# An mLSTM cell with a multiplicative FFN on one core: transposes of y, k and q moved from TensorE to VectorE

## Chip, cores, metric

One core of a Trainium2 chip. The metric is device time of one execution in microseconds (us), lower is better.

## The reference

```python
# mLSTM cell: batch 4, heads 8, 768 tokens, head dimension 40
for t in range(S):
    m_new = np.maximum(f_gate[:, :, t] + m, i_gate[:, :, t])
    C = f_stab * C + i_stab * (v_t outer k_t)        # state per batch and head
    n = f_stab * n + i_stab * k_t
    y[:, :, t] = sigmoid(o_gate_t) * (C @ q_t) / max(|n . q_t|, 1)
x = y.transpose(0, 2, 1, 3).reshape(3072, 320)
# multiplicative FFN, weights in float64
out = ((x @ w1) * (x @ w2) @ w3 @ w_out).astype(np.float32)   # (3072, 320)
```
(The stabilised gates are written in words.)

## The kernel before

The sequence is cut into 24 units of 128 rows of one batch. A loop of 30 steps runs the cell of unit s in step s; y of unit n is formed on VectorE right after the cell matmuls of step n+1, and turned (so that features lie on partitions) for the up-projections some steps later. Beside this, the float64 weights are converted by five VectorE passes a piece, two pieces a step; a piece of w3 is then transposed into `w3T`, and TensorE folds w3 and w_out into one matrix, one `wp` block a step in steps 10 to 17. Steps 17 to 26 each have two output blocks `po`.

TensorE does all transposes: `pt` for k and q, `px` for y.

```python
    def turn(n):                                   # k and q of unit n
        for src, dst, name in ((kbuf[n % NB], kT_t, "kT"), (qbuf[n % NBQ], qT_t, "qT")):
            pt = mps([128, NP, P], "pt")
            for p in range(NP):
                transpose(pt[:, p, :], src[:, 2 * p:2 * p + 2, :].rearrange("p a b -> p (a b)"))
            dst[n] = sb.tile([128, NP, P], FP, name=name, tag=name)
            nc.scalar.copy(out=dst[n], in_=pt)
    # ... cut
    def w3_mm(ko):                                 # one block of w3 times w_out
        w3T = w3T_t.pop(ko)
        wp = mps([128, DM], "wp")
        for ki in range(FO):
            mm(wp, w3T[:, ki, :], wo[:, ki, :], start=(ki == 0), stop=(ki == FO - 1))
        nc.scalar.mul(out=w3o[:, ko, :], in_=wp, mul=UP ** -2)
    # ... cut; the loop of steps, shortened:
    for s in range(len(n_up)):
        # loads for s+2 and s+3 on the SP queue
        if s < NU:
            # ...
            if s:
                turn(s)
        while turned < min(s - 2, NU):
            x_trans(turned)                        # px: y of unit s-3
            turned += 1
        fold()                                     # wp
        for _ in range(n_down[s]):
            ffn_out(*downs.pop(0))                 # po
        now = [ups.pop(0) for _ in range(n_up[s])]
        open_ups = [up(*x) for x in now]           # pa, pb
        if len(now) < 2 and turned == s - 2 < NU:
            x_trans(turned)
            turned += 1
        # ...
        quarter_work(s, rest)                      # ab; cell; pw, state, h, y
        # ...
        for _ in range(n_cvt[s] if s < len(n_cvt) else 0):
            convert()                              # five passes, then w3T
            converted += 1
        while todo and fetched < converted + (2 if s < 2 else 3):
            fetch(*todo.pop(0))                    # next raw weights, SP queue
            fetched += 1
```
TensorE's order is pinned to the order in which the program is written. VectorE's order is not, from step 7 on: the build places its instructions by its own estimate of when their inputs are there.

Of the kernel before, what the change touches and what calls it, by code (L numbers as in the profile page):

```python
# [8 lines left out]
FP = mybir.dt.float32  # L9
# [7 lines left out]
def kernel(  # L17
# [26 lines left out]
    nc = tc.nc  # L44
# [44 lines left out]
    def mm(out, lhsT, rhs, start=True, stop=True):  # L89
        in_order(nc.tensor.matmul(out, lhsT=lhsT, rhs=rhs, start=start, stop=stop))  # L90
# [3 lines left out]

    halves = [slice(0, L), slice(L, P)]
    quarters = ((0, 0), (1, 1), (0, 1), (1, 0))


    NB, NBQ = 4, 3
    qbuf = [const.tile([P, H, DP], FP, name=f"qbuf{i}") for i in range(NBQ)]  # L100
    kbuf = [const.tile([P, H, DP], FP, name=f"kbuf{i}") for i in range(NB)]
# [6 lines left out]
    decay = const.tile([P, B * NP, NT], FP, name="decay")  # L108
    U_d = dram.tile([NT, BH, L], FP, name="U_d")

    o_t, u_t = {}, {}

    def rows(src, n):
        c, b = divmod(n, B)
        return src[b, :, c * P:(c + 1) * P, :].rearrange("h p d -> p h d")

    def load(n):
        for dst, src in ((kbuf[n % NB][:, :, 0:D], k), (qbuf[n % NBQ][:, :, 0:D], q), (vbuf[n % NB][:, :, 0:D], v)):
            nc.sync.dma_start(out=dst, in_=rows(src, n))

# [145 lines left out]

    def turn(n):
        for src, dst, name in ((kbuf[n % NB], kT_t, "kT"), (qbuf[n % NBQ], qT_t, "qT")):
            pt = mps([128, NP, P], "pt")
            for p in range(NP):  # L270
# [3 lines that stand above are left out]
# [12 lines left out]
    def quarter_work(s, rest):  # L286
# [11 lines left out]
        if 0 <= n < NU:  # L298
            pw, vt, qT = u_t.pop(n), vbuf[n % NB], qT_t.pop(n)
            before = before_t.pop(n)  # L300
            for hd in range(H):
                for x, r in enumerate(halves):
                    mm(ph[x][:, hd, :], pw[r, hd, :], vt[r, hd, :])
            for p in range(NP):
                for hip, x in quarters:
                    mm(pi[halves[x], hip, p, :], qT[halves[hip], p, halves[x]], before[x][halves[hip], p, :])
        n, first_read = s, None
        if n < NU:
# [11 lines left out]
            for p in range(NP):  # L320
                for hip, x in quarters:
                    mm(ss[halves[x], hip, p, :], kT[halves[hip], p, halves[x]], qT[halves[hip], p, halves[x]])
            pv = pw.rearrange("p (n two) t -> p two n t", two=2)
# [10 lines left out]
        if 0 <= s - 1 < NU:  # L334
            if first_read is None:
                outputs(s - 1, pi, ph)
            else:
                with tc.issue_after(first_read.ins):
                    outputs(s - 1, pi, ph)

    def outputs(n, pi, ph):
# [6 lines left out]
        for x, r in enumerate(halves):  # L348
# [11 lines left out]
        y_t[n] = sb.tile([P, DM + REM], FP, name="y", tag="y")  # L360
        nc.vector.tensor_tensor(out=y_t[n][:, 0:DM].rearrange("p (h d) -> p h d", d=D), in0=h[:, :, 0:D], in1=e,  # L361
                                op=OP.mult)

    def twice(n):
# [15 lines left out]
    RG = GR * BH  # L380
    f_sb, a, F, U, on = (const.tile([RG, TC], FP, name=n) for n in ("f_sb", "a", "F", "U", "on"))
    w, g = f_sb, on
# [32 lines left out]
    for t in state:  # L415
        nc.gpsimd.memset(t[0], 0.0)
    nc.gpsimd.memset(pick, 0.0)

# [97 lines left out]
    def ffn_out(gr, j):  # L516
        po = mps([P, DM], "po")
        for f in range(FO):
            mm(po, ab_t[gr][j // 2][:, f, j % 2 * P:(j % 2 + 1) * P], w3o[:, f, :], start=(f == 0), stop=(f == FO - 1))
        o_sb = ffn.tile([P, DM], FP, name="o_sb", tag="o_sb", bufs=3)  # L520
        nc.scalar.copy(out=o_sb, in_=po)  # L521
        t0 = j * S + gr * P
        nc.sync.dma_start(out=out[t0:t0 + P, :], in_=o_sb)

# [14 lines left out]
    for s in range(len(n_up)):  # L539
# [8 lines left out]
        if s < NU:  # L548
            weighted(s)
            if s >= B:  # L550
                decayed(state[s % B][1], state[s % B][0], s, 0)
            if s:
                turn(s)
        if 0 <= s - 2 < NU:
            twice(s - 2)
        while turned < min(s - 2, NU):
            x_trans(turned)
            turned += 1
# [4 lines left out]
        open_ups = [up(*x) for x in now]  # L563
        if len(now) < 2 and turned == s - 2 < NU:
            x_trans(turned)
            turned += 1

        def rest():
            for x in open_ups:
                up_rest(*x)  # L570

        if s <= NU:
            quarter_work(s, rest)
        else:
            rest()
        if s == 0:
            gate_cols(g, gT, nc.scalar.copy)
            out_gate(0)
            scale_next()
            weights(1)  # L580
# [3 lines left out]
        if B - 1 <= s < NU:  # L584
            if s + 1 < NU:
                weights(s + 1)
            out_gate(s)
        for _ in range(n_cvt[s] if s < len(n_cvt) else 0):
            convert()
            converted += 1  # L590
        while todo and fetched < converted + (2 if s < 2 else 3):
# [35 lines left out]
```

## Time and profile before

| | before |
|---|---|
| time, median of 4 | 495.28 us (494.52 to 497.24) |
| TensorE busy | 462.7 us, 94% |
| VectorE busy | 247.5 us, 50% |
| a step in 12 to 16 | 16.77 us |
| a step in 18 to 23 | 21.08 us |

The prediction shows the lines that carry the bound. Two more are needed later: what the SP queue, which issues all but three of the transfers that the page lists (274 of 277), waits for. The columns are total us, times, longest us.

```profile
SPq L523 <- ACT o_sb L521: 166.7, 24, 30.8
...
SPq L154 <- DVE ma L173: 36.0, 13, 5.1
```
The first is output rows waiting for their copy, the second raw weights waiting for a buffer that a conversion pass must free.

### The profile page before, as it was taken

The numbers are of one execution on the slowest core, as the hardware profiler recorded it, in microseconds if no ns is written. First come the engines' busy times: TensorE is split into PE (matmuls) and PEld (weight loads), VectorE is DVE, ScalarE is ACT, GpSimd is POOL, SyncE is SP. The second block draws the span as 40 slices with busy tenths as digits, with TensorE's granted clock in tenths as the row PEclk, the third lists the DMA queues.
The fourth block names the chain that finished last, engine by engine and source line by source line (L and its number), as shares of the span: only waits on it lengthen the run. The fifth ranks groups of instructions, "written<-read, shape, count | busy, mean of one in ns | idle before, by whom it ended". The sixth has DMA issues, their size and how long they took to land.

```text
span 494.0 us, 13423 instructions
## 1 busy us (share of the span) xinstructions
PE 462.7 (94%) x5714; PEld 380.6 (77%) x5714; DVE 247.5 (50%) x512; ACT 153.5 (31%) x413; POOL 88.6 (18%) x163
## 2 busy tenths in 40 slices
PE   3869797899899999999999999999999998999997
PEld 2759796898677888788878787777878777777864
DVE  7787688999877978977431331403214042111110
ACT  3743454533431543354331322412112011011011
POOL 5431223621311322212410211201000000000000
PEclk9989998989999999999999999999999999999999
DMA  9999936799877737543340422311000000000001
GB/s 186 169 196 197 155 91 130 124 184 180 156 147 136 156 113 152 103 74 56 53 88 15 102 50 56 65 40 41 15 28 1 27 16 15 27 15 13 1 15 40
DMA packets 115404, 42.33 MB, mean 86 GB/s; under 512 B 103120, under 2 KB 106384, under 8 KB 115344
## 3 DMA queue, kind: packets, MB, share of 16 engines
q1 hardware_dynamic: 115200, 41.37, 41.9%
q8 instruction: 45, 0.74, 0.7%
q14 instruction: 15, 0.12, 0.1%
q10 hardware_dynamic: 144, 0.10, 0.1%
HBM read 37.42 MB, written 4.03 MB: 84 GB/s over the span
## 4 chain that ended last, share of the span: by engine, by line
PE 75%; DVE 9%; issue 7%; DMA 3%; SPq 2%; POOL 2%; ACT 1%; DVEq 0%; POOLq 0%; ACTq 0%
PE po L90 21%; PE pa L90 20%; PE pb L90 14%; PE cell L90 7%; PE wp L90 7%; PE pt L93 3%; SPq L154 2%; DVE h L349 1%; DMA raw<-in_moe_w_dram 1%; DMA pw<-U_d 1%; PE px L93 1%; DMA kbuf<-in_k_dram 1%; PE ub L90 1%; DVE h L345 1%; DVE ma L173 1%
## 5 line engine op out<-in xcount | busy, mean ns | idle before, releaser
L514 DVE TENSOR_TENSOR ab<-pb,a_sb 128x512 f32<-128x512 f32 x48 | 33.0, 690 | 182.0 <-ACT a_sb L513 181.9
L90 PE MATMUL po<-w3o,ab 128*128 128x320 f32 x384 | 105.4, 433 | 1.3 <-DVE h L349 1.3
L90 PEld LDWEIGHTS po<-w3o,ab 128*128 128x128 f32 x384 | 72.2, 190 | 30.7 <-issue 1.5
L90 PE MATMUL pa<-xT,w 128*128 128x256 f32 (+1 forms) x448 | 93.0, 355 | 0.0
L90 PE MATMUL pb<-xT,w 128*128 128x256 f32 (+1 forms) x448 | 91.9, 351 | 0.4 <-issue 0.4
L90 PEld LDWEIGHTS pa<-xT,w 128*128 128x128 f32 x448 | 77.1, 195 | 10.7 <-ACT a_sb L513 0.8
L90 PEld LDWEIGHTS pb<-xT,w 128*128 128x128 f32 x448 | 76.3, 192 | 9.0 <-issue 0.6
L513 ACT ACTIVATE a_sb<-pa 128x512 f32<-128x512 f32 x48 | 28.6, 596 | 146.6 <-PE pb L90 146.6
L90 PE MATMUL pb<-xT,wr 64*64 64x256 f32 (+1 forms) x448 | 47.4, 351 | 0.0
L90 PE MATMUL pa<-xT,wr 64*64 64x256 f32 (+1 forms) x448 | 47.4, 351 | 0.0
L283 POOL TENSOR_TENSOR state<-state,decay 128x164 f32<-128x164 f32 x40 | 19.6, 493 | 154.2 <-PE cell L90 99.1
L264 POOL TENSOR_SCALAR_AFFINE_SELECT pw<-pw 64x512 f32<-64x512 f32 x48 | 36.9, 769 | 47.1 <-ACT pw L262 44.6
L262 ACT ACTIVATE pw<-pw,aT 128x64 f32<-128x64 f32 x160 | 40.6, 339 | 5.3 <-DMA pw<-U_d 5.3
L90 PEld LDWEIGHTS pa<-xT,wr 64*64 64x64 f32 x448 | 28.5, 133 | 14.9 <-issue 6.6
L90 PE MATMUL wp<-wo,w3T 128*128 128x320 f32 x128 | 35.9, 433 | 2.0 <-DVE w3T L223 2.0
L521 ACT COPY o_sb<-po 128x320 f32<-128x320 f32 x24 | 10.2, 426 | 74.8 <-PE po L90 74.7
L90 PEld LDWEIGHTS wp<-wo,w3T 128*128 128x128 f32 x128 | 23.7, 190 | 11.1 <-issue 2.2
L90 PEld LDWEIGHTS cell<-vbuf,pw 64*64 64x64 f32 x768 | 28.2, 145 | 2.8 <-issue 0.3
L90 PEld LDWEIGHTS pb<-xT,wr 64*64 64x64 f32 x448 | 28.5, 133 | 0.0
L90 PE MATMUL cell<-vbuf,pw 64*64 64x41 f32 x768 | 28.4, 235 | 0.0
L365 POOL COPY y<-y 128x64 f32<-128x64 f32 x24 | 7.3, 306 | 110.0 <-DVE y L361 109.8
L324 DVE TENSOR_TENSOR pw<-cell,pw 128x512 f32<-128x512 f32 x24 | 16.4, 685 | 19.0 <-PE cell L90 15.4
(89 smaller groups left out, 524.4 us busy)
## 6 DMA issues: line engine op xcount, KB each, us to landing
raw<-in_moe_w_dram SPq DMA_DIRECT2D x64, 128.0 KB, 3.5
pw<-U_d SPq DMA_DIRECT2D x40, 128.0 KB, 3.7
kbuf<-in_k_dram SPq DMA_DIRECT2D x24, 160.0 KB, 4.6
qbuf<-in_q_dram SPq DMA_DIRECT2D x24, 160.0 KB, 4.9
vbuf<-in_v_dram SPq DMA_DIRECT2D x24, 160.0 KB, 4.9
o_in<-in_o_gate_dram SPq DMA_DIRECT2D x24, 160.0 KB, 4.1
out_dram<-o_sb SPq DMA_DIRECT2D x24, 160.0 KB, 1.8
raw<-in_moe_w_dram SPq DMA_DIRECT2D x7, 512.0 KB, 5.8
```

The costliest lines, as they stand in the source:

```text
L90: in_order(nc.tensor.matmul(out, lhsT=lhsT, rhs=rhs, start=start, stop=stop))
L93: in_order(nc.tensor.transpose(out, in_, ident[0:n, 0:n]))
L154: nc.sync.dma_start(out=dst, in_=src)
L173: V.scalar_tensor_tensor(out=r.bitcast(FP), in0=lo, scalar=2.0 ** -52, in1=r.bitcast(FP), op0=OP.mult, op1=OP.mult)
L262: nc.scalar.activation(out=pw[:, h, :], in_=src[:, h, :], func=AF.Exp, bias=aT[:, c, b * H + h:b * H + h + 1])
L264: nc.gpsimd.affine_select(out=pw[r], in_=pw[r], compare_op=OP.is_ge, fill=0.0, base=0, pattern=[[0, H], [1, L]], channel_multiplier=-1)
L283: nc.gpsimd.tensor_tensor(out=new, in0=old, op=OP.mult, in1=decay[:, b * NP:(b + 1) * NP, 2 * c + x:2 * c + x + 1] .to_broadcast([P, NP, D1]))
L324: first_read = nc.vector.tensor_tensor(out=pv, in0=ss, in1=pv, op=OP.mult)
L365: nc.gpsimd.tensor_copy(out=y_t[n][:, DM:DM + REM], in_=y_t[n][:, KF * P:DM])
L513: nc.scalar.mul(out=a_sb, in_=pa, mul=UP ** -2)
L514: nc.vector.tensor_tensor(out=ab_t[gr][j][:, fs[0]:fs[-1] + 1, t0:t0 + a_sb.shape[-1]], in0=pb, in1=a_sb, op=OP.mult)
L521: nc.scalar.copy(out=o_sb, in_=po)
```

## The change

The intent is to take transposes off TensorE, which is 94% busy, and put them on VectorE, which is half idle. The program has VectorE turn 32x32 blocks (the `r=32` of its rearrangements) and has the blocks moved by transfers: y of units 8 to 23 goes to DRAM and comes back as 32-row blocks, and k and q of units 17 to 23 are loaded that way. The conversion passes are told to follow the x transpose of their step. Output rows go to ScalarE's DMA queue. The diff, cut to its core:

```diff
+    N_DVE = 17
+    NY = 8
+    def send(n):                                  # y to DRAM: 4 DMAs on SP
+    def get_back(n):                              # back as 32-row blocks: 4 DMAs on SP
+        back_t[n] = sb.tile([P, 4, KC, 32], FP, name="yb", tag="yb", bufs=1)
+    def x_turn(n):
+        return nc.vector.transpose(out=x_t[gr][...], in_=back_t.pop(n)...)
     def turn(n):
+        if n >= N_DVE:                            # k, q by VectorE
+            nc.vector.transpose(out=dst[n]..., in_=src[...]...)
+            return
-                    mm(pi[...], qT[halves[hip], p, halves[x]], before[x][halves[hip], p, :])
+                    mm(pi[...], qT[heads[hip], p, halves[x]], before[x][heads[hip], p, :])   # 40 rows, not 64
-        nc.sync.dma_start(out=out[t0:t0 + P, :], in_=o_sb)
+        nc.scalar.dma_start(out=out[t0:t0 + P, :], in_=o_sb)
-        if 0 <= s - 2 < NU:
-            twice(s - 2)
+        if NY <= s - 2 < NU:
+            send(s - 2)
+        elif 0 <= s - 2 < NY:
+            twice(s - 2)
+        if N_DVE <= s + 1 < NU:
+            load_turned(s + 1)
+        if NY <= s - 2 < NU:
+            get_back(s - 2)
-        if len(now) < 2 and turned == s - 2 < NU:
+        if len(now) == 1 and turned == s - 2 < NY:
-            quarter_work(s, rest)
+            gated = quarter_work(s, rest)         # returns the instruction y
+        with tc.issue_after(gated.ins) if gated else nullcontext():
+            if NY <= s - 2 < NU:
+                gated = x_turn(s - 2)
+            if N_DVE <= s + 1 < NU:
+                turn(s + 1)
-        for _ in range(n_cvt[s] if s < len(n_cvt) else 0):
-            convert()
+        with tc.issue_after(gated.ins) if gated else nullcontext():
+            for _ in range(n_cvt[s] if s < len(n_cvt) else 0):
+                convert()
```
`issue_after` keeps what stands in it behind the named instruction. `o_sb` goes from 3 to 2 buffers.

More of the change, by code (lines that the diff above doesn't have):

```diff
@@ L1 @@
-from contextlib import ExitStack
+from contextlib import ExitStack, nullcontext
 import concourse.bass as bass
@@ L95 @@
     halves = [slice(0, L), slice(L, P)]
+    heads = [slice(0, D), slice(DP, DP + D)]
     quarters = ((0, 0), (1, 1), (0, 1), (1, 0))
     NB, NBQ = 4, 3
+    N_DVE = 17
     qbuf = [const.tile([P, H, DP], FP, name=f"qbuf{i}") for i in range(NBQ)]
@@ L109 @@
     U_d = dram.tile([NT, BH, L], FP, name="U_d")
+    NY = 8
+    KC = KF + 1
+    y_d = [dram.tile([P, 4, KC, 32], FP, name=f"y_d{n}") if n >= NY else None for n in range(NU)]
     o_t, u_t = {}, {}
@@ L118, in load, with load_turned @@
         for dst, src in ((kbuf[n % NB][:, :, 0:D], k), (qbuf[n % NBQ][:, :, 0:D], q), (vbuf[n % NB][:, :, 0:D], v)):
-            nc.sync.dma_start(out=dst, in_=rows(src, n))
+            if src is not q or n < N_DVE:
+                nc.sync.dma_start(out=dst, in_=rows(src, n))
+    def load_turned(n):
+        c, b = divmod(n, B)
+        for dst, src in zip(turned_in, (k, q)):
+            for hip in range(2):
+                of = src[b].rearrange("(p two) s d -> two p s d", two=2)[hip, :, c * P:(c + 1) * P, :]
+                for j in range(2):
+                    p0, c0 = hip * DP + j * 32, (1 - j) * 32
+                    nc.sync.dma_start(out=dst[p0:p0 + 32, c0:c0 + NP * RAW].rearrange("r (p e) -> r p e", p=NP),
+                                      in_=of.rearrange("p (r f) d -> r p (f d)", f=4))
     def load_o(n):
@@ L267, in turn @@
     def turn(n):
+        if n >= N_DVE:
+            for src, dst, name in zip(turned_in, (kT_t, qT_t), ("kT", "qT")):
+                dst[n] = sb.tile([128, NP, P], FP, name=name, tag=name)
+                nc.vector.transpose(out=dst[n].rearrange("i p (r f) -> i p f r", f=4),
+                                    in_=src[:, 32:TB].rearrange("i (p f d) -> i p f d", p=NP, f=4)[:, :, :, 0:32])
+            return
         for src, dst, name in ((kbuf[n % NB], kT_t, "kT"), (qbuf[n % NBQ], qT_t, "qT")):
@@ L305, in quarter_work @@
                 for hip, x in quarters:
-                    mm(pi[halves[x], hip, p, :], qT[halves[hip], p, halves[x]], before[x][halves[hip], p, :])
+                    mm(pi[halves[x], hip, p, :], qT[heads[hip], p, halves[x]], before[x][heads[hip], p, :])
         n, first_read = s, None
@@ L321, in quarter_work @@
                 for hip, x in quarters:
-                    mm(ss[halves[x], hip, p, :], kT[halves[hip], p, halves[x]], qT[halves[hip], p, halves[x]])
+                    mm(ss[halves[x], hip, p, :], kT[heads[hip], p, halves[x]], qT[heads[hip], p, halves[x]])
             pv = pw.rearrange("p (n two) t -> p two n t", two=2)
@@ L335, in quarter_work @@
             if first_read is None:
-                outputs(s - 1, pi, ph)
-            else:
-                with tc.issue_after(first_read.ins):
-                    outputs(s - 1, pi, ph)
+                return outputs(s - 1, pi, ph)
+            with tc.issue_after(first_read.ins):
+                return outputs(s - 1, pi, ph)
     def outputs(n, pi, ph):
@@ L360, in outputs @@
         y_t[n] = sb.tile([P, DM + REM], FP, name="y", tag="y")
-        nc.vector.tensor_tensor(out=y_t[n][:, 0:DM].rearrange("p (h d) -> p h d", d=D), in0=h[:, :, 0:D], in1=e,
+        return nc.vector.tensor_tensor(out=y_t[n][:, 0:DM].rearrange("p (h d) -> p h d", d=D), in0=h[:, :, 0:D], in1=e,
                                 op=OP.mult)
+    def send(n):
+        y = y_t.pop(n)
+        for cc in range(KF):
+            nc.sync.dma_start(out=y_d[n][:, :, cc, :], in_=y[:, cc * P:(cc + 1) * P].rearrange("t (i c) -> t i c", c=32))
+        for i in range(0, 4, 2):
+            nc.sync.dma_start(out=y_d[n][:, i:i + 2, KF, :], in_=y[:, KF * P:DM].rearrange("t (i c) -> t i c", c=32))
+    back_t = {}
+    def get_back(n):
+        back_t[n] = sb.tile([P, 4, KC, 32], FP, name="yb", tag="yb", bufs=1)
+        for i in range(4):
+            nc.sync.dma_start(out=back_t[n][32 * i:32 * (i + 1)].rearrange("r m k c -> r m (k c)"),
+                              in_=y_d[n][:, i].rearrange("(m r) k c -> r m (k c)", r=32))
+    def x_turn(n):
+        gr, j = divmod(n, GT)
+        if j == 0:
+            x_t[gr] = ffn.tile([128, KC, TG], FP, name="xT", tag="xT")
+        return nc.vector.transpose(out=x_t[gr][:, :, j * P:(j + 1) * P].rearrange("c k (m r) -> c k m r", r=32),
+                            in_=back_t.pop(n).rearrange("r m k c -> r k m c"))
     def twice(n):
@@ L380 @@
     RG = GR * BH
-    f_sb, a, F, U, on = (const.tile([RG, TC], FP, name=n) for n in ("f_sb", "a", "F", "U", "on"))
+    RAW = 4 * D
+    TB = 32 + NP * RAW
+    gates = const.tile([P, 2 * TB], FP, name="gates")
+    f_sb, a, F, U, on = (gates[0:RG, i * TC:(i + 1) * TC] for i in range(5))
+    turned_in = [gates[:, i * TB:(i + 1) * TB] for i in range(2)]
     w, g = f_sb, on
@@ L416 @@
         nc.gpsimd.memset(t[0], 0.0)
+    nc.gpsimd.memset(gates[:, 5 * TC:2 * TB], 0.0)
+    nc.gpsimd.memset(gates[RG:P, NP * RAW:TB], 0.0)
     nc.gpsimd.memset(pick, 0.0)
@@ L519, in ffn_out @@
             mm(po, ab_t[gr][j // 2][:, f, j % 2 * P:(j % 2 + 1) * P], w3o[:, f, :], start=(f == 0), stop=(f == FO - 1))
-        o_sb = ffn.tile([P, DM], FP, name="o_sb", tag="o_sb", bufs=3)
+        o_sb = ffn.tile([P, DM], FP, name="o_sb", tag="o_sb", bufs=2)
         nc.scalar.copy(out=o_sb, in_=po)
         t0 = j * S + gr * P
-        nc.sync.dma_start(out=out[t0:t0 + P, :], in_=o_sb)
+        nc.scalar.dma_start(out=out[t0:t0 + P, :], in_=o_sb)
     ups = [(0, list(range(f, f + 4)), slice(j * P, (j + 1) * P)) for f in (0, 4) for j in range(GT)]
@@ L551 @@
                 decayed(state[s % B][1], state[s % B][0], s, 0)
-            if s:
+            if 0 < s < N_DVE:
                 turn(s)
-        if 0 <= s - 2 < NU:
+        if NY <= s - 2 < NU:
+            send(s - 2)
+        elif 0 <= s - 2 < NY:
             twice(s - 2)
-        while turned < min(s - 2, NU):
+        if N_DVE <= s + 1 < NU:
+            load_turned(s + 1)
+        if NY <= s - 2 < NU:
+            get_back(s - 2)
+        while turned < min(s - 2, NY):
             x_trans(turned)
@@ L570, in rest @@
                 up_rest(*x)
+        gated = None
         if s <= NU:
-            quarter_work(s, rest)
+            gated = quarter_work(s, rest)
         else:
             rest()
+        with tc.issue_after(gated.ins) if gated else nullcontext():
[3 more added lines that the diff above has]
+                turn(s + 1)
         if s == 0:
@@ L587 @@
             out_gate(s)
-        for _ in range(n_cvt[s] if s < len(n_cvt) else 0):
-            convert()
-            converted += 1
+        with tc.issue_after(gated.ins) if gated else nullcontext():
+            for _ in range(n_cvt[s] if s < len(n_cvt) else 0):
+                convert()
+                converted += 1
         while todo and fetched < converted + (2 if s < 2 else 3):
```

## The prediction

> **What bounds the kernel now.** I read the page first: busy time, slices, chain of waits.
>
> ```profile
> PE 462.7 (94%) x5714; PEld 380.6 (77%) x5714; DVE 247.5 (50%) x512; ACT 153.5 (31%) x413; POOL 88.6 (18%) x163
> ...
> PE   3869797899899999999999999999999998999997
> ...
> DVE  7787688999877978977431331403214042111110
> ```
>
> A slice is 12.35 us. TensorE (PE) is full from slice 11 on; VectorE (DVE) is 70 to 90% busy up to slice 18 and idle after. Next, the chain in order of time; two stretches give the cost of each piece, start to start:
>
> ```profile
> 162.99 1.02 PE pt L93 x8
> 164.34 4.31 PE wp L90 x16
> 168.65 1.73 PE pa L90 x8
> ...
> 177.44 2.32 PE cell L90 x123
> 179.76 1.02 PE pt L93 x8
> ...
> 272.23 1.02 PE pt L93 x8
> 273.58 8.62 PE po L90 x32
> ...
> 293.31 1.02 PE pt L93 x8
> 294.66 8.62 PE po L90 x32
> ```
>
> The eight k/q transposes of a step (pt) cost 1.02 us; they end at 164.01 and wp starts at 164.34, so the three y transposes (px) between cost 0.33. I number steps by the loop; the first wp (w3 times w_out) is in step 10, so the pt at 162.99 opens step 12's work. A step there is 16.77 us (162.99 to 179.76): pt 1.02, px 0.33, and 15.42 of wp, up-projections and cell. From step 18 a step is 21.08. Nothing else stands on this path after 147 us.
>
> Before that TensorE is not full. Its timeline shows the waits and their price:
>
> ```profile
> 33.80 0.88 PE L93 MATMUL px<-ident,y 128*128 128x128 f32 x3 [4.06 <-DVE y L361]
> ...
> 59.57 0.29 PE L90 MATMUL cell<-vw,kbuf 64*64 64x41 f32 x3 [2.09 <-issue]
> ...
> 60.78 1.11 PE L93 MATMUL pt<-ident,kbuf 128*128 128x128 f32 x4
> ...
> 129.19 4.54 PE L90 MATMUL wp<-wo,w3T 128*128 128x320 f32 x16 [1.98 <-DVE w3T L223]
> ```
>
> The last line matters most: wp waits for VectorE's converted and transposed w3. VectorE's timeline shows how tight that is:
>
> ```profile
> 134.80 0.43 DVE L170 TENSOR_SCALAR ex<-raw 128x512 uint32<-128x512 uint32 x1 [1.49 <-ACT raw L159]
> ...
> 137.90 0.71 DVE L223 STREAM_TRANSPOSE w3T<-w 128x512 f32<-128x512 f32 x1
> 138.54 0.38 DVE L170 TENSOR_SCALAR ex<-raw 128x512 uint32<-128x512 uint32 x1
> 138.96 0.69 DVE L171 SCALAR_TENSOR_TENSOR ex<-raw,ex 128x512 uint32<-128x512 uint32 x1
> 142.34 0.69 DVE L514 TENSOR_TENSOR ab<-pb,a_sb 128x512 f32<-128x512 f32 x1 [2.70 <-ACT a_sb L513]
> 142.95 0.42 DVE L172 TENSOR_SCALAR ma<-ex 128x512 uint32<-128x512 uint32 x1
> ```
>
> One conversion with its transpose is 3.74 us (134.80 to 138.54); two are needed per wp. At 142.34 a pass that was ready (L172) stood behind an ab that was not[...].
>
> [...] Here, after 2.09 us idle, four transposes took 1.11 us against 0.66 in full flow, and at 33.80, after 4.06 idle, three took 0.88 against 0.49. [...] The w3T transpose of 128x512 here takes 0.71 us. [...] The waits of the SP queue agree: 166.7 us behind o_sb, with loads queued after it. That is why the output rows go to ScalarE's queue.
>
> **The change part by part.**
>
> Removed from TensorE: px for 16 units, 16 x 0.33 = 5.3 us, all in the full stretch; pt for 7 units (17 to 23), 7 x 1.02 = 7.1. Together 12.4. Their ScalarE copies (16 of 0.49, 14 of 0.59) go too and were beside the path.
>
> Moved: the first px goes from step 2 to step 3, so its 4.06 us wait vanishes. VectorE's next cell read then starts when its conversion ends (36.6) instead of at 39.22; I take 2.6 us, if the DVE-bound stretch after it keeps the shift.
>
> Added on VectorE: 16 transposes of 128x384. Estimate from w3T's 0.71 us for 512: about 0.6 each. And 14 of 128x512, 0.71 each, after step 16 where VectorE is under half busy: hidden.
>
> Added on the SP queue: 8 transfers per y and 8 per turned k/q, estimated at the 0.5 to 0.6 us issue of today's loads: 4.5 and then 9 us per step, beside 16 to 20 us steps. The DRAM round trip (two landings of some 2 to 5 us) fits too: y is there at the start of a step, x is wanted a step later. From step 17 on I expect no new wait.
>
> Reordered: this is the dear part. The passes are now to follow the step's y transpose. The built program shows what the scheduler made of it. The y transpose of step 10 did not go behind step 10's y but a whole step later, and the passes of step 10 stand behind it:
>
> ```
> before: y(9) | passes | ab(11) passes ab passes | cell(11): pw ... y(10)
> after:  y(9) | ab(11) ab | cell(11): pw ... y(10) | xT | 12 passes (w3T w3T) | ab(12) xT ...
> ```
>
> So up to step 11 VectorE idles from y(9) to ab(11), and the two w3T that wp of step 12 reads come only behind the cell of step 11. Let T be that cell's end on TensorE. VectorE's cell work pw to y takes 5.0 us (165.62 to 170.57 before), xT 0.6, two conversions 7.5: w3T is ready at T+13.1. TensorE wants it after pt, T+1.0. Stall 12.1 us.
>
> The next steps repeat it in part, as ab of step s stands ahead of half of the passes that wp of step s+1 needs. With ab at 2.4 us before the end of the cell, I walk the order:
> - step 13: ab, xT, pass, ab, four passes end 2.5 after the cell; pw, w3T, then five passes and w3T mixed with state and h: 9.1. Stall 8.1.
> - step 14: three passes and w3T between and behind the ab, two more, pw, then the rest mixed: 7.3. Stall 6.3.
> - steps 15 and 16 repeat the two patterns: 8.1 and 6.3.
> - step 17: its passes fit ahead of ab(16): no stall.
>
> Sum 40.9 us. [...] the pieces after 33.80 and 59.57 took some 2 us longer than in full flow, so 5 x 2 = 10.
>
> Sum: 494.7 - 12.4 - 2.6 + 40.9 + 10 = 530.6. The terms most likely too high are the cold ones; I say 528.
>
> **The rivals.** First, all is hidden: the passes find their slot and only TensorE's gain remains, 494.7 - 12.4 - 2.6 = 480, 3% faster. For it: VectorE has the throughput (some 15 us of work in 16.4 us steps). Against: throughput is not order, and the order is fixed in the program. Second, SP becomes the bound[...]. That would show as late kbuf, yb or turned tiles, some 5 to 15 us more, mostly in steps 10 to 16. For it: the SP queue already waits 36 us for conversions to free raw tiles. Against: in my walk its loads are still a dozen us early. It would come on top: 535 to 545. Third, the late steps lose: the turned k/q land after VectorE wants them and ab queues behind; each late us would repeat in 8 steps. Slack there is about 8 us, so I give it little.
>
> **Range and chances.** If the stalls are two thirds of my walk and half the cold cost is real, 494.7 - 15 + 27 + 5 = 512; with the SP rival, 540. Faster needs the walk to be wrong in kind: 6%. Within 2% (485 to 505): 6%. Slower: 88%.
>
> **What would show it.** TensorE waits of about 12, 8, 6, 8, 6 us in front of wp in steps 12 to 16, released by VectorE's w3T, with a lowered clock in those slices; steps of 25 to 30 us there, and of 19.7 us (21.08 - 1.35) from step 18 on; px and pt groups down to 24 and 136 instructions. Wrong would be: waits at wp under 3 us each, or the loss lying in front of pt, pa or the cell, or released by DMA; or late steps still near 21 us.

494.7 - 12.4 - 2.6 + 40.9 + 10 = 530.6, rounded down to 528. What the trace of the kernel before shows:
- The pass L172 had its input at 139.65 us (L171, 138.96 + 0.69) and started at 142.95, behind the ab that VectorE had waited 2.70 us for. That VectorE would keep the built order in the same way elsewhere, on which the walk of the stalls rests, was the premise; order_alone below tests it.
- The granted clock was 0.50 from about 32.4 us, within the wait of 4.06 that ended at 33.80, to 39.2, and from about 59.7, as the wait of 2.09 ended, to 63.1. "Cold" stands for such work at a granted clock of 0.50. That each of the five stalls would have it behind it was the estimate from these two places.
- The SP queue waited 166.7 us for `o_sb` and 36.0 for raw buffers; that what is queued behind a waiting transfer waits too was a premise, here and for the SP rival (early_order below shows one case).

## The result

542.68 us median of 4 (539.09 to 543.67) against 495.28. Ratios here are the mean time of one kernel's fast runs over that of the other's of the same rounds, so not quite the ratio of the medians: 1.0933, 95% interval 1.0879 to 1.0986. That is slower, as forecast, but outside the range of 512 to 540.

The page of the changed kernel, in the parts that the prediction read first, with the clock that TensorE was granted:

```profile
PE 466.1 (87%) x5610; PEld 377.4 (70%) x5610; DVE 269.8 (50%) x542; ACT 140.6 (26%) x383; POOL 83.3 (15%) x149
...
PE   3899879896992776776768999999999999999997
...
DVE  7888799897637255445457605325415413310210
...
PEclk9669989897997696978798999999999999999999
```
A slice is now 13.4 us. TensorE has a trough in slices 13 to 22, counted from 1 (about 161 to 296 us; the prediction counts from 0), where it was full before, and the granted clock dips in the same slices (its mean from 163.8 to 300.8 us is 0.81, and 1.00 after). It also dips in slices 2 and 3, to 0.6, which matters at the end. Its timeline names the wait; after the matmuls' start, duration and shapes, the bracket gives the idle time before them and what ended it:

```profile
128.34 6.86 PE L90 MATMUL wp<-wo,w3T 128*128 128x320 f32 x16 [4.34 <-DVE w3T L239]
178.46 7.39 PE L90 MATMUL wp<-wo,w3T 128*128 128x320 f32 x16 [13.61 <-DVE w3T L239]
205.93 7.31 PE L90 MATMUL wp<-wo,w3T 128*128 128x320 f32 x16 [7.94 <-DVE den L377]
231.73 6.36 PE L90 MATMUL wp<-wo,w3T 128*128 128x320 f32 x16 [6.36 <-DVE w3T L239]
258.17 6.79 PE L90 MATMUL wp<-wo,w3T 128*128 128x320 f32 x16 [7.94 <-DVE den L377]
283.74 5.96 PE L90 MATMUL wp<-wo,w3T 128*128 128x320 f32 x16 [6.64 <-DVE w3T L239]
```
The first line is step 10's. The waits of steps 12 to 16 are 13.61, 7.94, 6.36, 7.94 and 6.64: 42.5 us. The five blocks take 33.8 us where five in full flow (4.47 in this view) take 22.4: 11.5 us more. Windows of half a microsecond show the granted clock at 0.50 up to about 184.2 us, 5.7 us into the block of step 12, and at 1.00 after. VectorE's timeline shows the cause of the first wait:

```profile
161.33 0.69 DVE L568 TENSOR_TENSOR ab<-pb,a_sb 128x512 f32<-128x512 f32 x1 [8.67 <-ACT a_sb L567]
...
163.91 0.69 DVE L348 TENSOR_TENSOR pw<-cell,pw 128x512 f32<-128x512 f32 x1 [0.85 <-PE cell L90]
...
169.94 0.49 DVE L384 TENSOR_TENSOR y<-h,o_in 128x320 f32<-128x320 f32 x1
170.35 0.57 DVE L408 STREAM_TRANSPOSE xT<-yb 128x384 f32<-128x384 f32 x1
170.85 0.38 DVE L186 TENSOR_SCALAR ex<-raw 128x512 uint32<-128x512 uint32 x1
...
177.60 0.71 DVE L239 STREAM_TRANSPOSE w3T<-w 128x512 f32<-128x512 f32 x1
194.52 0.69 DVE L568 TENSOR_TENSOR ab<-pb,a_sb 128x512 f32<-128x512 f32 x1 [16.21 <-ACT a_sb L567]
```
VectorE idles 8.67 us before the ab of step 11 with step 10's passes still to do: they stand behind y and the x transpose (170.35) in its order. The second w3T runs at 177.60, and wp starts at 178.46.

After step 17 the picture turns. The chain of the work that ended last, in order of time, one whole late step:

```profile
300.81 4.50 PE wp L90 x16
...
322.73 2.32 PE cell L90 x123
325.04 8.81 PE po L90 x32
333.86 1.73 PE pa L90 x8
...
342.65 2.32 PE cell L90 x123
```
From cell to cell it is 19.92 us (322.73 to 342.65) where it was 21.08: the 1.35 of pt and px is gone, and po takes 8.81 instead of 8.62.

It pays to cut the span at two marks that all kernels have: the start of step 12 on TensorE, and the start of the wp of step 17. The first part then holds VectorE's busy early stretch, the second the five steps in question, the third the late steps.

| kernel (profiled run) | start to step 12 | step 12 to wp of step 17 | from there to the end | span |
|---|---|---|---|---|
| before | 162.9 | 85.1 | 246.0 | 494.0 |
| after | 163.8 | 137.0 | 236.7 | 537.4 |

So +0.8, +51.9 and -9.3 make the difference of 43.4 us. The loss lies wholly in the five steps.

### The profile page after: what moved, and what is told of

Its sections match the earlier page's. It is cut to its first block, busy times and chain, and to the rows that moved or that the text cites. A ratio compares the mean times of both kernels' runs of the same rounds, so it can differ in the third digit from the quotient of the medians.

```text
span 537.4 us, 13428 instructions
## 1 busy us (share of the span) xinstructions
PE 466.1 (87%) x5610; PEld 377.4 (70%) x5610; DVE 269.8 (50%) x542; ACT 140.6 (26%) x383; POOL 83.3 (15%) x149
## 2 busy tenths in 40 slices
DMA packets 151005, 52.07 MB, mean 97 GB/s; under 512 B 131552, under 2 KB 141984, under 8 KB 150944
## 4 chain that ended last, share of the span: by engine, by line
PE 64%; issue 14%; DVE 12%; POOL 4%; DMA 4%; SPq 1%; ACT 1%; POOLq 0%; DVEq 0%
PE po L90 20%; PE pa L90 17%; PE pb L90 12%; PE wp L90 8%; PE cell L90 5%; POOL state L307 2%; DMA vbuf<-in_v_dram 2%; DVE h L372 1%; DVE ma L189 1%; POOL pw L280 1%; DMA raw<-in_moe_w_dram 1%; DVE w L190 1%; DMA kbuf<-in_k_dram 1%; DVE ma L188 1%; DVE ab L568 1%
## 5 line engine op out<-in xcount | busy, mean ns | idle before, releaser
L90 PE MATMUL wp<-wo,w3T 128*128 128x320 f32 x128 | 49.7, 557 | 46.8 <-DVE w3T L239 31.0
L90 PEld LDWEIGHTS wp<-wo,w3T 128*128 128x128 f32 x128 | 31.5, 253 | 62.6 <-issue 35.4
L307 POOL TENSOR_TENSOR state<-state,decay 128x164 f32<-128x164 f32 x40 | 20.7, 518 | 221.1 <-PE cell L90 73.0
L280 POOL TENSOR_SCALAR_AFFINE_SELECT pw<-pw 64x512 f32<-64x512 f32 x48 | 35.3, 736 | 61.5 <-ACT pw L278 59.9
L575 ACT COPY o_sb<-po 128x320 f32<-128x320 f32 x24 | 10.2, 423 | 76.6 <-PE po L90 76.4
L175 ACT ACTIVATE raw<-raw 128x512 f32<-128x512 f32 (+1 forms) x32 | 19.8, 635 | 26.0 <-DVE w L190 11.1
L372 DVE TENSOR_TENSOR h<-cell,h 64x328 f32<-64x328 f32 x48 | 23.8, 495 | 1.0
```

The costliest lines, as they stand in the source:

```text
L90: in_order(nc.tensor.matmul(out, lhsT=lhsT, rhs=rhs, start=start, stop=stop))
L175: nc.scalar.mul(out=hi, in_=hi, mul=2.0 ** -111)
L280: nc.gpsimd.affine_select(out=pw[r], in_=pw[r], compare_op=OP.is_ge, fill=0.0, base=0, pattern=[[0, H], [1, L]], channel_multiplier=-1)
L307: nc.gpsimd.tensor_tensor(out=new, in0=old, op=OP.mult, in1=decay[:, b * NP:(b + 1) * NP, 2 * c + x:2 * c + x + 1] .to_broadcast([P, NP, D1]))
L372: nc.vector.tensor_tensor(out=h[r], in0=ph[x], in1=h[r], op=OP.add)
L575: nc.scalar.copy(out=o_sb, in_=po)
```

## The experiments

**Theory A:** the loss is the place of the passes in VectorE's order, and the slow clock behind each stall (0.50 at the start of each of the five blocks). **B:** SP's queue and the trip through DRAM. **C:** VectorE has too much to do. I ran 15 kernels; the kernel before ran at a median of 495.5 to 496.7. All outputs are right. All runs are in the table at the end of this section.

### behind_y: the passes follow y, not the x transpose

```diff
-                gated = x_turn(s - 2)
+                x_turn(s - 2)
```

> One line of the changed kernel is undone: the conversion passes of a step follow that step's y, as they would with no x transpose there, and no longer the x transpose. All transfers, all VectorE transposes and their number stay. Theory A (the loss is the place of the passes in VectorE's order, with the slow clock that follows each stall): the five wp waits of steps 12 to 16 (42.5 us in all) shrink to under 3 us each and their wp blocks go back to 4.3 to 4.5 us, so some 54 us come back: 487 to 491 us. Theory B (SP's queue, the trip through DRAM and its traffic cost the time): nothing of that is changed, so over 530. Theory C (VectorE has too much to do in steps 10 to 17): the work is the same, so over 525.

Measured: 508.51 us (505.09 to 509.50), ratio to before 1.026. One line gives back 34 us; nothing of the transfers or of VectorE's work changed, so B and C can't be the main cause. But I had expected 487 to 491. TensorE's timeline shows what took the place of the old waits:

```profile
183.21 4.55 PE L90 MATMUL wp<-wo,w3T 128*128 128x320 f32 x16 [1.70 <-DVE w3T L239]
192.41 3.45 PE L90 MATMUL pa<-xT,w 128*128 128x256 f32 x8 [4.66 <-DVE xT L408]
...
234.32 3.75 PE L90 MATMUL pa<-xT,w 128*128 128x256 f32 x8 [4.66 <-DVE xT L408]
```
In steps 13 and 15 the up-projection waits for x. VectorE is busy with passes right up to these x transposes (191.73 and 233.64 us, no idle time before them), so x is late by its place in VectorE's order, and not by its transfers. In the changed kernel that lateness had been hidden under the waits for w3T.

### free_passes: the passes tied to nothing

```diff
-        with tc.issue_after(gated.ins) if gated else nullcontext():
+        with nullcontext():
             for _ in range(n_cvt[s] if s < len(n_cvt) else 0):
```

> The changed kernel with the passes tied to nothing, as before the change; transfers and transposes stay. A: as behind_y, and besides, the early loss between steps 8 and 11 (3.7 us, where wp of step 10 waited 4.34 us) goes if it came from holding the passes behind y: 483 to 487, some 3 to 4 us under behind_y. If the early loss has another cause: equal to behind_y within 1 us. B and C: over 525.

Measured: 501.48 (501.00 to 502.96), ratio 1.012. The middle part is 97.7 us against behind_y's 102.2, but its early part was 3.0 longer (166.9 against 164.0), so the gap of 7 us in the medians says nothing about the early loss. That expectation failed; the waits for x (3.59 and 3.49 us) remain.

### order_alone: the changed kernel's VectorE order, without the change

`ORDER` lists VectorE's instructions of steps 10 to 16 by their number in the program, as the build of the changed kernel had arranged them, less the x transposes.

```diff
-    NY = 8
+    NY = NU                                       # y stays on TensorE
-    N_DVE = 17
+    N_DVE = NU                                    # k and q too
     behind.close()
+    dve = [i for i in traced() if i.engine == mybir.EngineType.DVE]
+    for x, y in zip(ORDER, ORDER[1:]):            # order only, no wait is added
+        tc.add_manual_dep(dve[y], dve[x].name, ...)
```

> The opposite test: y stays on TensorE for all 24 units, k and q too, so there is no trip through DRAM for y, no block loads and no transpose of x, k or q on VectorE; but VectorE's instructions of steps 10 to 16 are held in the very order that the changed kernel's build gave them, less the x transposes. A: the stalls come back whole, with nothing of the late gain: 495 + 53 + 1 = about 549 us (540 to 552). B and C: near the kernel before, 488 to 500 us.

Measured: 556.98 (555.69 to 559.13), ratio 1.124. Without any trip, block load or x transpose the whole loss is there, and the same waits:

```profile
183.32 6.84 PE L93 MATMUL wp<-wo,w3T 128*128 128x320 f32 x16 [13.50 <-DVE w3T L242]
212.06 6.13 PE L93 MATMUL wp<-wo,w3T 128*128 128x320 f32 x16 [9.44 <-DVE den L380]
...
264.65 7.13 PE L93 MATMUL wp<-wo,w3T 128*128 128x320 f32 x16 [8.04 <-DVE den L380]
```
The middle part is 140.5 us (138.1 expected: 85.1 + 53), the late one 246.1 as before. The rest of the 8 us above my 549 is its early part of 168.4. The order is enough to make the loss. The run order_only below is this same kernel without the held order, and takes 500.65: the order alone costs 56.3 us.

### warm and warm2: TensorE kept busy in the stalls

```diff
         wp = mps([128, DM], "wp")
+        for _ in range(WARM.get(ko, 0)):          # overwritten by the true ones
+            mm(wp, w1[:, 0, 0:128], wo[:, 0, :])
```
with VectorE's order held as in the changed kernel, and WARM 50, 29, 23, 29, 24 for steps 12 to 16.

> The changed kernel with VectorE's order held as it is there, and TensorE kept busy in the five stalls: 50, 29, 23, 29 and 24 matmuls of 128x128 by 128x320 that need nothing from VectorE run into wp's own PSUM tile ahead of the true ones, which overwrite them. At 0.27 us each (4.31 us for 16) they fill 13.5, 7.8, 6.2, 7.8 and 6.5 us. The result stays right. If what the five slow wp blocks cost (7.39, 7.31, 6.36, 6.79, 5.96 us against 4.31 each, 12.3 us in all) is the clock that falls while TensorE idles, the wp blocks take 4.3 to 4.5 us and the time falls by 10 to 12 us, to 530 to 533. If they are slow for another reason (operands, banks), the time stays at 541 to 544.

Measured: 571.09 (567.90 to 571.29). This missed because I had counted wrongly: each filler is two instructions in the trace (50 gave x100), so they filled twice the time. With 41.8 us too many and the wp blocks at 4.47 (11.5 us less in all) the sum is 542.7 - 11.5 + 41.8 = 573. The run was repeated with half the fillers.

> The run warm again with the right number of fillers: each filler was two instructions of 0.27 us, not one, so warm filled 83.6 us instead of 41.8 (572 by that sum, measured 571). Now 25, 14, 11, 14 and 12 fillers, that is 13.5, 7.6, 5.9, 7.6 and 6.5 us. With the clock theory of the slow wp blocks: wp at 4.3 to 4.6 us and 10 to 12 us off the changed kernel: 530 to 533. Otherwise 541 to 544.

Measured: 531.38 (529.48 to 534.67), 11.3 us under the changed kernel. The fillers of step 12 and the true blocks of steps 12 and 13:

```profile
168.53 13.62 PE L93 MATMUL wp<-wo,w 128*128 128x320 f32 x50
182.21 4.57 PE L93 MATMUL wp<-wo,w3T 128*128 128x320 f32 x16
...
206.78 4.57 PE L93 MATMUL wp<-wo,w3T 128*128 128x320 f32 x16 [0.31 <-DVE den L384]
```
With TensorE busy ahead of it a block takes 4.57 us instead of 7.39, at a granted clock of 1.00 (windows 168 to 182 and 182 to 187 us) instead of 0.50 for the first 5.7 us. The middle part falls from 137.0 to 125.5 us, which is the 11.5 that the slow blocks had cost. So of the loss some 11 us is the clock and the rest the waits.

### kq_only and order_only: no y through DRAM; no k, q either

```diff
-    NY = 8
+    NY = NU
```
for kq_only; order_only has N_DVE = NU besides.

> The changed kernel with y left to TensorE for all 24 units (no trip through DRAM); k and q of units 17 to 23 are still turned by VectorE and the passes stand behind y. If what behind_y still lost (17 us over my forecast) is x arriving late by the trip (its profile shows two waits of 4.66 us of the up-projection on x in steps 13 and 15), it is gone here: 494.7 - 7 x 1.02 = 487.6, give or take 3 us of the early stretch: 485 to 491. If the residue is in the passes behind y, or in the k/q loads and transposes, it stays: 500 or more.

Measured: 493.91 (491.01 to 496.36), ratio 0.996. The middle part is 84.2 and the late one 240.6: both waits for x are gone, so behind_y's residue belonged to y's way through DRAM and VectorE. The miss has no seen cause: the traced execution (491.01 us, the fastest) lies at the edge of the range, and the slower ones have no trace.

> As kq_only, but k and q stay on TensorE too. What is left of the change: first y transposes a step later, passes behind that step's y, output rows on ScalarE's queue, 40 rows instead of 64 in the cell's matmuls. Expected: the kernel before within the early stretch's spread, 492 to 498, and kq_only 7.1 us below it. If holding the passes behind y costs in steps 12 to 16, over 500.

Measured: 500.65 (499.68 to 502.88), ratio 1.009. Middle 85.1, late 245.9: as before to 0.1 us. So the output rows' new queue and the 40-row matmuls change nothing in those parts, and neither do passes behind y. The 6.7 us between the medians of the two kernels is close to the 7.1 of k and q; in the traces the middle and late parts differ by 0.9 and 5.3, and the early parts by 5.6 more (170.1 against 164.5), though both kernels do the same there. In the trace the miss is all early.

### early_send: y sent a step sooner

`send` and `get_back` of unit s-1 move to the end of step s, ahead of the next step's loads; the passes are tied to nothing.

> A repair: passes tied to nothing, and y is sent to DRAM and fetched back at the end of the step that makes it, ahead of the next step's loads in the SP queue, so that x can be turned a step sooner (the build then puts the transpose of x of unit 8 right behind y of unit 9, a step earlier than in the changed kernel). If the residue is x coming late, both waits for x in steps 13 and 15 go, steps 12 to 16 take 16.4 us each, and the late gain stays: 494.7 - 1.7 - 9.5 = 483.5, give or take 3 of the early stretch: 481 to 488. If the trip's traffic or SP's issues are the limit, it stays at 498 to 503 as free_passes.

Measured: 499.60 (496.95 to 503.52), ratio 1.007: a miss. No wait for x is left, but the build now put the second w3T behind the ab of the next step, and wp waited 1.5 to 1.7 us in each of steps 12 to 16, with slow blocks of up to 6.24 us behind. The middle part stayed at 98.2.

### given_order: the changed kernel, VectorE in program order

```diff
     behind.close()
+    dve = [i for i in traced() if i.engine == mybir.EngineType.DVE]
+    for x, y in zip(ORDER, ORDER[1:]):
+        tc.add_manual_dep(dve[y], dve[x].name, ...)
```
with `ORDER = range(246, 413)`: nothing but the order in which the program writes VectorE's instructions of steps 10 to 15.

> The changed kernel, every line of it, with one thing added: VectorE's instructions of steps 10 to 15 are held in the order in which the program writes them (x transpose, the twelve passes, then the next step's ab), where the build had moved them. Transfers, SP's queue and all work are those of the changed kernel. Theory A in its second form (behind_y and early_send stayed 15 us too slow because their x or their second w3T still stood in a bad place, not because the trip is slow): steps 12 to 16 take 16.4 to 16.8 us each and step 17 24.3, so 161.2 us of steps 12 to 17 become about 106: 485 to 491 us. If the trip through DRAM or SP's queue is too slow for a step, VectorE waits at the x transpose ahead of the passes, and steps 12 to 16 stay at 18 to 20 us: 498 or more.

Measured: 495.42 (493.27 to 498.46), ratio 0.999. Holding the order, with every transfer and every instruction of the changed kernel kept, removes 47.3 us, the whole loss. It doesn't reach the expected 485 to 491. VectorE's timeline has the remainder:

```profile
176.13 0.49 DVE L387 TENSOR_TENSOR y<-h,o_in 128x320 f32<-128x320 f32 x1
180.67 0.58 DVE L411 STREAM_TRANSPOSE xT<-yb 128x384 f32<-128x384 f32 x1 [4.05 <-DMA yb<-y_d]
184.23 0.71 DVE L242 STREAM_TRANSPOSE w3T<-w 128x512 f32<-128x512 f32 x1
188.07 0.71 DVE L242 STREAM_TRANSPOSE w3T<-w 128x512 f32<-128x512 f32 x1
```
The x transpose now stands ahead of the passes and waits 4.05 us for its blocks; five such waits in a row are 2.5 to 4.3 us long. Here rival B shows: the middle part is 90.1 us, where fetch_first below needs 82.4.

### early_order, best_px2, px_alone

early_order is early_send with VectorE's order held: first piece and w3T, x transpose, second piece and w3T, both ab.

> early_send (y sent and fetched a step sooner) with VectorE's order held too: first pass and w3T, x transpose, second pass and w3T, then both ab. Expected under A: the waits of 1.7 us for the second w3T and the slow wp blocks behind them (3.4 us a step in early_send) go: 16.4 us a step, 499.6 - 13 = 486, 483 to 490; equal to given_order within 3 us if the trip fits either way.

Measured: 505.75 (503.35 to 508.19), ratio 1.020: worse, not better. One line tells why:

```profile
172.09 0.54 DVE L411 STREAM_TRANSPOSE xT<-yb 128x384 f32<-128x384 f32 x1
178.34 0.43 DVE L189 TENSOR_SCALAR ex<-raw 128x512 uint32<-128x512 uint32 x1 [5.71 <-ACT raw L178]
```
The next piece of w3 is not there. SP fetches it behind the get-back; the get-back needs `yb`, which has one buffer and is free only when the x transpose before it has run; that x transpose now stands behind a pass. In SP's timeline the get-back starts at 172.65, as the x transpose ends (172.09 + 0.54), the other seven raw transfers of the step are issued behind it from 174.44 to 177.69, and the pass starts at 178.34. The queue ties the passes and the transposes together. That the queue causes this wait is read from the code and the trace; fetch_first, below, tests it. No run has a second `yb` buffer.

best_px2 is early_order with `len(now) < 2`, the first px back in step 2.

> early_order with the first y transpose put back into step 2, as in the kernel before. In the profiles so far step 2 and 3 together take 20.65 us in the kernel before; with the transpose in step 3 they take 18.1 to 18.5 [...] and 22 to 22.6 [...]. So this should be level with early_order or up to 2 us faster: 482 to 488.

Measured: 507.32 (504.21 to 508.53), ratio 1.022, level with early_order; its base was wrong, and so was the number.

px_alone is the kernel before with that one condition changed:

```diff
-        if len(now) < 2 and turned == s - 2 < NU:
+        if len(now) == 1 and turned == s - 2 < NU:
```

> The kernel before with only the first y transpose moved from step 2 to step 3. My prediction took 2.6 us off for this. From the spread of steps 2 and 3 in the profiles (18.3 or 22.3 against 20.65) it should be no gain: 492 to 498, within 0.6% of the kernel before, with single runs 4 us apart. If the move is worth what I said: 492.1.

Measured: 494.40, single runs from 491.08 to 498.11, ratio 0.998 (0.991 to 1.006). Its middle and late parts are those of the kernel before (85.1 and 246.0). The 2.6 us that I had booked can't be told from nothing.

### fetch_first, fetch_first_free, late_y: the queue repaired

After 12 runs this was open: why the change gains nothing once the order is repaired. fetch_first puts the w3 fetches ahead of the trip of y at the end of a step, and holds VectorE's order as y, both pieces with w3T, x transpose, both ab.

```diff
-        if NY <= s - 2 < NU:
-            send(s - 2)
-        elif 0 <= s - 2 < NY:
+        if 0 <= s - 2 < NY:
             twice(s - 2)
-        if NY <= s - 2 < NU:
-            get_back(s - 2)
...
-        with tc.issue_after(gated.ins) if gated else nullcontext():
+        with nullcontext():
             # passes
             fetch(*todo.pop(0))
             fetched += 1
+        if s <= NU and NY <= s - 1 < NU:
+            send(s - 1)
+            get_back(s - 1)
```

> The order of SP's queue and of VectorE repaired together: w3 pieces are fetched first, then y is sent and fetched back, at the end of the step; VectorE's order is held as y, twelve passes, x transpose, ab, ab. Then neither the passes nor the x transpose should wait: steps 12 to 16 take 16.4 to 16.8 us (given_order 18.1 on average, early_order 20.1), step 17 24.3, and the late steps 19.92: 495.4 - 9 = 486, 483 to 490. If something else in the trip costs (traffic, SP's issues of 12 us a step), the steps stay at 18 us and the time at 494 or more.

(The 12 us of SP's issues: in early_order's SP timeline those from 149.48 to 163.29 us take 12.1.)

Measured: 485.22 (484.02 to 486.58), ratio 0.979 (0.972 to 0.986): the fastest of all, as forecast (whether by a full 2% the interval leaves open). In steps 12 to 16 neither the passes nor the x transpose wait, and no wp does:

```profile
174.85 0.71 DVE L242 STREAM_TRANSPOSE w3T<-w 128x512 f32<-128x512 f32 x1
175.49 0.54 DVE L411 STREAM_TRANSPOSE xT<-yb 128x384 f32<-128x384 f32 x1
176.18 0.69 DVE L571 TENSOR_TENSOR ab<-pb,a_sb 128x512 f32<-128x512 f32 x1 [0.15 <-ACT a_sb L570]
```

```profile
163.09 4.47 PE L93 MATMUL wp<-wo,w3T 128*128 128x320 f32 x16
...
212.59 4.47 PE L93 MATMUL wp<-wo,w3T 128*128 128x320 f32 x16
229.03 4.47 PE L93 MATMUL wp<-wo,w3T 128*128 128x320 f32 x16
```
The middle part is 82.4 us, 2.7 under the kernel before. Its edit keeps every transfer of the changed kernel (52.07 MB in that kernel's page), so the amount of traffic is not what made the changed kernel slower.

fetch_first_free leaves VectorE's order to the build.

> fetch_first with VectorE's order left to the build, which then puts the second pass and the second w3T behind the first ab, and the x transpose between h and the denominators. If order matters to the last pass, wp waits 1 to 2 us for the second w3T in most of steps 12 to 16 and runs cold behind it, 2 to 3.5 us a step: 496 to 503. If not, equal to fetch_first.

Measured: 490.22 (489.56 to 491.24), ratio 0.988. No wp of steps 12 to 16 waits; instead the first pa of steps 13 and 15 waits 1.55 us until VectorE is at the denominators, right behind the x transpose in that order. So even with the queue repaired the build's order costs 5 us, less than I said and in front of another block.

late_y has NY = 16 in the changed kernel: y takes the trip only after the last conversion.

> y goes through DRAM only from unit 16 on, when the last conversion is over; k and q as in the changed kernel. Steps 12 to 16 should be those of kq_only (16.77 us), and the late steps 19.92 to 20.2: 493.9 - 8 x 0.28 = 491.7, 488 to 495; against the kernel before it saves 7 x 1.02 + 8 x 0.33 = 9.8 less some 2 of the early stretch. If the y trip costs by itself, over 496.

Measured: 489.25 (488.44 to 490.81), ratio 0.987. Middle 84.2, late 237.2. One constant away from the changed kernel, and the x transpose no longer meets the passes.

All runs; the parts are those of the profiled execution, the time is the median:

| kernel | to step 12 | 12 to wp of 17 | to the end | time | ratio |
|---|---|---|---|---|---|
| order_alone | 168.4 | 140.5 | 246.1 | 556.98 | 1.124 |
| warm | 163.9 | 165.7 | 236.6 | 571.09 | 1.150 |
| warm2 | 167.6 | 125.5 | 236.9 | 531.38 | 1.071 |
| behind_y | 164.0 | 102.2 | 237.2 | 508.51 | 1.026 |
| free_passes | 166.9 | 97.7 | 236.6 | 501.48 | 1.012 |
| best_px2 | 165.3 | 102.7 | 238.8 | 507.32 | 1.022 |
| early_order | 159.9 | 102.6 | 239.5 | 505.75 | 1.020 |
| early_send | 164.1 | 98.2 | 239.4 | 499.60 | 1.007 |
| order_only | 170.1 | 85.1 | 245.9 | 500.65 | 1.009 |
| given_order | 169.9 | 90.1 | 236.7 | 495.42 | 0.999 |
| px_alone | 159.8 | 85.1 | 246.0 | 494.40 | 0.998 |
| kq_only | 164.5 | 84.2 | 240.6 | 493.91 | 0.996 |
| fetch_first_free | 163.7 | 87.3 | 237.7 | 490.22 | 0.988 |
| late_y | 165.6 | 84.2 | 237.2 | 489.25 | 0.987 |
| fetch_first | 162.2 | 82.4 | 238.1 | 485.22 | 0.979 |

## Why the prediction was right and wrong

The direction and the mechanism held; the size did not, and 542.7 lies outside 512 to 540. Three terms of the sum were mis-sized: the moved px (2.6 us booked as a gain; the early part came out 0.8 us longer), the cold blocks with the rounding down, and, least, the stalls.

**The stalls** were right: forecast 12.1, 8.1, 6.3, 8.1, 6.3 (40.9 us), measured 13.61, 7.94, 6.36, 7.94, 6.64 (42.5), with the releaser that the prediction named or, twice, the next instruction of VectorE. order_alone and given_order show the cause from both sides.

**The cold term** failed in its reading: "The terms most likely too high are the cold ones; I say 528." They were too low. Forecast 10, measured 11.5, and warm2 gave 11.3 back. Rounding the sum of 530.6 down to 528 went the wrong way by 2.6.

**The moved px** is the term that failed most: "I take 2.6 us, if the DVE-bound stretch after it keeps the shift." It doesn't. At step 6 the changed kernel was ahead (VectorE read the cell at 81.10 us against 84.42), and it still was when step 10 began on TensorE (122.57 against 125.79), but at step 12 it was 0.8 behind, a miss of 3.4. The trace shows where the lead went: the wp of step 10 waited 4.34 us instead of 1.98, and ran 6.86 instead of 4.54 (granted clock 0.50 from 128.4 to 133.0 us; in the kernel before 1.00 over the whole block). So the lead was lost at a place that the walk of the reordering left out: it counted stalls only from step 12 on, and tying the passes to y already lengthened the wait of step 10. Where the passes follow y before step 10, that wp waits 2.2 to 4.5 us (all 9 profiles of this kind); where they are free, it waits 1.98 (all 8, the kernel before included). The slow block is not due to the tie alone: it takes 6.23 or 6.24 in six of these 8 too. px_alone, the move by itself, can't tell a gain of 2.6 from none. The early part varies from 159.8 to 170.1 us between profiles of kernels that are nearly alike in it; the granted clock there varies, too (mean up to 162.9 us: 0.95 in the kernel before, 0.90 in the changed one), and I haven't settled what sets it.

**TensorE's gain** was right: 9.3 us after the wp of step 17, where the forecast's 12.4 less the five px and the pt and px ahead of that wp (3.0) makes 9.4.

**The remainder**: for the middle part the forecast amounts to 40.9 + 10 - 3.0 = 47.9, measured 51.9. Of these 4.0, 1.6 are the stalls and 1.5 the cold blocks; 0.9 is not traced. So 2.6 (rounding) + 4.0 (middle) + 3.4 (early) bring 528 to 538. The profiled execution took 539.1; the sum starts from 494.7, and the profiled execution of the kernel before took 495.7. The median is 3.6 us over that execution; only one execution has a trace, and the spread of the early part would do it, but that isn't shown.

**The range** was too narrow above. I had put its edge at the SP rival's 535 to 545 cut to 540, and left no room for the early stretch. The rivals: that all is hidden was wrong. SP as the bound was wrong for this kernel, though its queue waits rose:

```profile
SPq L170 <- DVE ma L189: 71.1, 13, 18.0
...
SPq L392 <- DVE xT L408: 52.2, 4, 15.2
```
Raw weights waited 71.1 us for the delayed passes (36.0 before): a result of the stalls. Once the stalls were gone, the same queue was the next limit (in given_order and early_order). So that rival was second in line, not on top as the prediction had it. The turned k and q took 1.08 us each on VectorE, not 0.71, and cost nothing; the late steps are 19.92 us against my 19.73, as po took 0.19 more.

## What to carry to other kernels

Giving an idle engine more work was not free here: the order of its instructions alone cost 56.3 us (order_alone against order_only). So look at the built order and ask, for each consumer on the critical engine, what stands ahead of its producer and what that waits for. Here the build moved the x transpose, which is fed by the trip through DRAM (in given_order VectorE waited up to 4.3 us for its blocks), by a whole step, and everything tied behind it moved along. When a repair brings less than forecast, look for the next wait in the trace; here the order of VectorE and the order of the DMA queue had to be repaired together before 10.2 of the 12.4 us taken off TensorE came through (fetch_first, 485.22 against 495.47).

## What the traces show of TensorE's clock and VectorE's transposes

- Windows of half a microsecond show the granted clock of the changed kernel at 0.50 at the start of each wp block of steps 12 to 16, and at 1.00 some 5.7, 5.6, 3.7, 4.6 and 2.9 us into it. The blocks took 2.92, 2.84, 1.89, 2.32 and 1.49 us more than 4.47, about half of these times. In the changed kernel's early stretch the granted clock stayed at 0.50 for 18 us (18 to 36) although TensorE was nearly always busy, with small matmuls:

```profile
21.00:24.00 3.00, 2.89 (x24) 2.22 (x24) 2.84 (x4) 2.26 (x10) 2.75 (x4) 0.50 0.70 112
24.00:27.00 3.00, 3.00 (x102) 3.00 (x104) 2.66 (x4) 1.45 (x3) 1.41 (x2) 0.50 1.13 160
27.00:30.00 3.00, 3.00 (x60) 2.76 (x55) 1.50 (x4) 0.30 (x2) 0.46 (x1) 0.50 0.91 211
```
  (Windows of 3 us: length, busy time with count of TensorE, its weight loads, VectorE, ScalarE, GpSimd, then the granted clock, DMA share, GB/s.) What held it in this stretch the runs don't show.
- VectorE's transposes in f32: 128x384 took 0.57 us in the changed kernel, 128x512 0.71, and the turned k and q, 128x512 with an interleaved output, 1.08 each.
